# Fourier mixing and balanced experts: x in runs of four rows, table phases on GpSimd, the last fold and the weight turns in pieces, two more pauses, an earlier gather

## The chip, the cores and the metric

The kernel runs on one core of a Trainium2 chip. The metric is the time of one execution on the device in microseconds (us). The kernel before takes 534.44 us (median of three runs, 532.58 to 536.25). With one core there is no other core of the run to compare with, so a run counts as slow only where it is over 1.5% above the fastest of the same kernel in the same rounds; a single look (experiments 5, 6 and 10 to 12) has no known state. Ratios below are the mean time of one kernel's fast runs over that of the other's of the same rounds, so they are not quite the ratio of the medians that stand beside them.

The runs fell on several chips. On four occasions the kernel before took 534.4 to 535.6 us, on four others 585.9 to 591.9 us. In the traces that I compared PE is as busy on the second kind up to about 300 us and less busy after it: from 200 to 300 us it is busy for 97.17 us in experiment 1 on such a chip and 96.86 in the kernel before on one of the first kind, from 300 to 400 us 90.17 and 99.50, at a granted clock of 0.965 and 0.969 over the whole run. I call them quick and slow chips, use ratios within the same rounds alone, and read the first 172 us of profiles from either kind.

## The reference

```python
X = np.fft.fft(x, axis=1)            # x: (8, 2496, 256) float32
X = np.fft.fft(X, axis=2).real       # (19968 tokens, 256)
logits = X @ w_gate                  # 8 experts, each with room for 19968/8 tokens
# greedy: the largest logit first, one expert a token, no expert over its room
for idx in argsort(-logits.flatten()): ...
# per expert: out[mask] = relu(X[mask] @ w1[e]) @ w2[e]      (F = 1024)
```

## The kernel before

The transform is a product with cosine and sine tables. Rows s and S - s of x are added first (the fold), so that half a table is enough. The reversed rows come by indirect loads, which GpSimd issues. One pass of the loop below is a batch; the tables are built beside it, one of ten sets (cosine and sine) at a time. In the timelines below an engine takes its instructions in the order in which they stand in the program (DVE's eleven from 44.13 us on, in the prediction, do).

```python
def load_x(b):                               # three tiles of each kind
    ...                                      # forward rows, by SyncE, two rows (2 KiB) a piece
    for i in range(NK):                      # NK = 5 indirect loads a batch
        nc.gpsimd.indirect_dma_start(out=bv[0:n, i, :], in_=x_pairs, ...)

def phases(w, row, turns, period):           # angle r = k*row - period*round(k*turns)
    nc.vector.tensor_scalar(n1, in0=kgrid[:, 0:w], scalar1=turns, scalar2=MAGIC, ...)
    nc.vector.tensor_scalar(n1, in0=n1, scalar1=MAGIC, scalar2=-float(period), ...)
    nc.vector.scalar_tensor_tensor(r_t, in0=kgrid[:, 0:w], scalar=row, in1=n1, ...)

for b in range(B):                           # B = 8
    nc.vector.tensor_tensor(a_t[...], a_t[...], b_t[..., reversed], op=AL.add)   # the fold
    if b + 3 < B: load_x(b + 3)              # waits for the fold: same tile
    if b > 0: tab_waves()                    # ACT: Abs, Sin, cast to bf16 (hi) from r_t
    nc.scalar.copy(zb[:, :, 0:D:P], ...)
    nc.vector.tensor_tensor(zb[...], ...)    # the two additions into zball
    zts[b] = [turn_x(b, pv, 0), turn_x(b, pv, 1)]     # PE transposes, ACT copies them out
    if b > 0: gate_x(b - 1, ...)             # PE: gate matmuls of the batch before
    ...
    tab_low()                                # DVE: lo = tf - hi
    tab_phases()                             # the next set of phases
# then logits; choice of the experts beside the transforms; experts; out by indirect scatters
```

## Time and profile before

| stage of the profiled run before | us |
|---|---|
| start to start of last fold | 77.1 |
| last fold to first transform matmul | 23.4 |
| to first matmul of the experts | 71.5 |
| to the end of GpSimd's last scatter | 357.0 |
| to the end of the program | 5.2 |
| span | 534.3 |

### The profile page before, as it was taken

How to read it: one execution, taken by the hardware profiler on the slowest of the kernel's cores; microseconds unless marked ns; L12 is line 12 of the kernel's file. 1: busy time of each engine (PE TensorE's matmuls, PEld its weight loads, DVE VectorE, ACT ScalarE, POOL GpSimd, SP SyncE). 2: the span in 40 equal slices, each digit the busy share in tenths (PEclk: the TensorE clock that was granted, in tenths of full speed). 3: DMA queues.
4: the chain of work that ended last, by engine and by line, in shares of the span. 5: the costliest groups of instructions: out<-in, count | busy, mean ns of one | idle time of the engine just before them, and what ended most of it. 6: DMA issues, size and time to landing. Idle time of an engine off the chain costs nothing.

```text
span 534.3 us, 11232 instructions
## 1 busy us (share of the span) xinstructions
PE 471.8 (88%) x4039; PEld 357.7 (67%) x4039; DVE 372.7 (70%) x952; ACT 337.9 (63%) x762; POOL 313.9 (59%) x362
## 2 busy tenths in 40 slices
PE   0567659899789899999899999999999999999983
PEld 0544436776568566777667877777777777777753
DVE  7799994687978969889978757566654555555431
ACT  7879983156368778788767776556555555555531
POOL 7888815253122555555524336777677777777774
PEclk9968898999989999999989999999999999999988
DMA  8999929078578697523322323342222222222221
GB/s 259 317 281 319 310 89 159 2 240 291 140 217 261 161 225 163 137 95 103 99 76 100 99 88 102 113 130 85 82 83 78 79 87 84 79 69 78 77 77 53
DMA packets 35168, 74.62 MB, mean 140 GB/s; under 512 B 6115, under 2 KB 14349, under 8 KB 35104
## 3 DMA queue, kind: packets, MB, share of 16 engines
q0 software_dynamic: 23296, 42.10, 30.2%
q1 hardware_dynamic: 11808, 31.73, 17.7%
q8 instruction: 33, 0.54, 0.4%
q14 instruction: 31, 0.25, 0.2%
HBM read 51.26 MB, written 32.24 MB: 156 GB/s over the span
## 4 chain that ended last, share of the span: by engine, by line
PE 70%; DVE 13%; ACT 9%; issue 4%; DMA 3%; POOL 1%; POOLq 0%; DVEq 0%; ACTq 0%
PE hps L1234 24%; PE ops L1257 24%; PE sps L1098 5%; PE fftps L1038 5%; PE wps L1058 2%; PE tp L285 2%; ACT zt L287 2%; DMA xa<-in_x_dram 2%; PE yps L295 1%; ACT tf L254 1%; POOL out_dram L1261 1%; DVE xa L343 1%; PE inv_ps L766 1%; DVE stage L1022 1%; PE tp L1222 1%
## 5 line engine op out<-in xcount | busy, mean ns | idle before, releaser
L995 ACT ACTIVATE hb<-hps 128x384 bf16<-128x384 f32 (+1 forms) x326 | 146.2, 493 | 50.5 <-PE hps L1234 47.4
L1257 PE MATMUL ops<-w2t,hb 128*128 128x256 bf16 (+1 forms) x1344 | 175.3, 274 | 0.0
L1257 PEld LDWEIGHTS <-hb 128*128 128x128 bf16 (+1 forms) x1344 | 133.3, 100 | 32.6 <-issue 0.5
L1261 POOL DMA_INDIRECT out_dram<-zball,rid x85 | 89.3, 1051 | 82.7 <-ACT zball L995 63.8
L1234 PE MATMUL hps<-xs,zball 128*128 128x384 bf16 x640 | 127.3, 327 | 0.0
L1234 PEld LDWEIGHTS <-zball 128*128 128x128 bf16 x896 | 86.1, 98 | 43.4 <-issue 2.9
L999 DVE TENSOR_SCALAR hb<-hps 128x384 bf16<-128x384 f32 (+1 forms) x122 | 66.3, 549 | 47.2 <-PE hps L1234 39.2
L129 POOL DMA_INDIRECT xb<-in_x_dram,mir_i x40 | 54.3, 1357 | 11.9 <-issue 10.5
L995 ACT ACTIVATE zball<-ops 128x256 f32<-128x256 f32 (+1 forms) x79 | 30.4, 384 | 31.6 <-PE ops L1257 29.0
L1234 PE MATMUL hps<-xt,zball 128*128 128x384 bf16 (+1 forms) x256 | 48.4, 322 | 0.0
L285 PE MATMUL tp<-identf,xa 128*128 128x128 f32 x160 | 27.4, 336 | 20.1 <-issue 9.2
L285 PEld LDWEIGHTS tp<-identf,xa 128*128 128x128 f32 x160 | 23.6, 176 | 27.1 <-issue 10.2
L995 ACT ACTIVATE xs<-sps 128x384 bf16<-128x384 f32 x68 | 30.4, 493 | 16.0 <-PE sps L1098 15.7
L1026 POOL COPY stage<-stage 128x258 bf16<-128x258 bf16 x40 | 17.7, 447 | 36.3 <-DVE stage L1021 33.0
L1098 PE MATMUL sps<-pt,xl 128*128 128x192 bf16 x320 | 33.8, 246 | 0.7 <-DVE pt L1076 0.7
L1076 DVE TENSOR_SCALAR pt<-rampw,spot 128x193 bf16<-128x193 bf16 x160 | 32.5, 298 | 1.6 <-PE inv_ps L766 0.9
L1098 PEld LDWEIGHTS <-xl 128*128 128x128 bf16 x320 | 27.6, 98 | 3.5 <-issue 1.6
L1210 POOL DMA_INDIRECT xg<-t_dram,ids_l x24 | 23.1, 964 | 7.3 <-issue 7.3
L1261 POOL DMA_INDIRECT out_dram<-zball,rows_l x23 | 22.3, 969 | 7.3 <-issue 2.4
L1044 ACT COPY ev<-fftps 128x512 f32<-128x512 f32 x20 | 11.7, 584 | 22.9 <-PE fftps L1038 15.5
L1001 DVE COPY zball<-ops 128x256 f32<-128x256 f32 (+1 forms) x29 | 12.3, 424 | 19.4 <-PE ops L1257 19.4
L1024 ACT ACTIVATE stage<-stage 128x254 bf16<-128x254 bf16 x40 | 15.6, 414 | 13.3 <-DVE stage L1021 11.6
(356 smaller groups left out, 781.1 us busy)
## 6 DMA issues: line engine op xcount, KB each, us to landing
t_dram<-stage SPq DMA_DIRECT2D x20, 512.0 KB
xl<-t_dram SPq DMA_DIRECT2D x20, 512.0 KB
xa<-in_x_dram SPq DMA_DIRECT2D x8, 1024.0 KB
w1raw<-in_moe_w_dram POOLq DMA_DIRECT2D x8, 512.0 KB, 5.3
w2t<-in_moe_w_dram POOLq DMA_DIRECT2D x8, 512.0 KB, 6.3
xa<-in_x_dram SPq DMA_DIRECT2D x8, 224.0 KB
out_dram<-zball,rid POOLq DMA_INDIRECT x85, 2.5
xb<-in_x_dram,mir_i POOLq DMA_INDIRECT x40, 8.0
```

The lines of the kernel that those rows point to most:

```text
L129: nc.gpsimd.indirect_dma_start(out=bv[0:n, i, :], out_offset=None, in_=x_pairs, in_offset=bass.IndirectOffsetOnAxis(ap=mir_i[0:n, b * NK + ...
L285: nc.tensor.transpose(tp[:, blk, u, :], pv[:, 4 * c + u, blk * P:(blk + 1) * P], identf)
L995: nc.scalar.activation(dst, src, ACT.Relu if relu else ACT.Copy)
L999: nc.vector.tensor_scalar(dst, in0=src, scalar1=0.0, scalar2=None, op0=AL.max)
L1026: nc.gpsimd.tensor_copy(st[:, :, 1 + q, 0:P + 1], st[:, :, 3 * q, 0:P + 1])
L1038: nc.tensor.matmul(fps[:, :, d0:d1], lhsT=tab[:nv, i, ks], rhs=zball[:nv, b0:b0 + NB, 2 * i + r, d0:d1], start=(i == 0), stop=(i == NK - 1))
L1076: nc.vector.tensor_scalar(marks[n][:, f, 0:EW + 1], in0=rampw[:, 0:EW + 1], scalar1=spot[:, c:c + 1], scalar2=None, op0=AL.is_equal)
L1098: nc.tensor.matmul(sps[:, j2 * EW:(j2 + 1) * EW], lhsT=xl[:, 2 * g + cc, j2 * P:(j2 + 1) * P], rhs=pt[:, 2 * g + cc, 0:EW], start=(cc == 0 ...
L1210: nc.gpsimd.indirect_dma_start(out=xg[0:nr, q, :], out_offset=None, in_=t_dram, in_offset=bass.IndirectOffsetOnAxis(ap=d["ids"](q, nr), ax ...
L1234: nc.tensor.matmul(hps[:, 0:n], lhsT=w1t[d["e"]][:, j2, fc * P:(fc + 1) * P], rhs=d["x"](j2), start=(j2 == 0), stop=(j2 == 1))
L1257: nc.tensor.matmul(ops[0:nr, 0:D], lhsT=d["hid"][:, fc, b0:b0 + nr], rhs=w2t[d["e"]][:, fc, :], start=(fc == 0), stop=(fc == F // P - 1))
L1261: put = nc.gpsimd.indirect_dma_start(out=out, out_offset=bass.IndirectOffsetOnAxis(ap=d["rows"](b0 // P)[0:nr], axis=0), in_=ot[0:nr, :], ...
```

## The change

The intent is to unload the two fullest units of the first stage (DVE, and GpSimd with its loads), to take serial work from the last fold, and to remove single stops of PE later. The core of the diff:

```diff
+    x_quads = x.rearrange("b (s r) d -> (b s) (r d)", r=4)
-        for i in range(NK):
+        for i in range(3):                       # two of 128 runs of four rows, one of 112 pairs
...
-    def phases(w, row, turns, period):
+    def phases(w, row, turns, period, eng=nc.vector):
-        nc.vector.tensor_scalar(n1, ...)          # twice
+        eng.tensor_scalar(n1, ...)                # twice
+        if eng is nc.vector:
+            eng.scalar_tensor_tensor(r_t, ...)
+        else:
+            eng.tensor_scalar(r_t, in0=kgrid[:, 0:w], scalar1=row, scalar2=None, op0=AL.mult)
+            eng.tensor_tensor(r_t, r_t, n1, op=AL.add)
...
+                                         nc.vector if len(tabq) > 5 else nc.gpsimd)))   # last six sets
...
+        for g0, g1 in ((0, 4), (4, 8), (8, 2 * NK)) if b == B - 1 else ((0, 2 * NK),):   # last fold
...
+        if b == B - 1:
+            gate_x(b - 1, zts.pop(b - 1))         # ahead of the last transposes
...
-            if clock["n"] in (18, 22, 28, 34):
-                turn_w((18, 22, 28, 34).index(clock["n"]), "A")
+            if clock["n"] in TURNS:               # 16 places, one piece each
+                next(pieces)
...
+        yield SYNC                                # one more pause before count()
...
+        yield from settle(1)                      # and one in the first settling
...
-        while ... j >= min(max(placed[0] + 1 + m * (51 - placed[0]) // 15, ...), 38 + m):
+        while ... j >= min(max(placed[0] + 1 + m * (50 - placed[0]) // 15, ...), 37 + m):
```

More of the change, by code (lines that the diff above doesn't have):

```diff
@@ L104 @@
     ab = {}
-    mir_i = const.tile([P, B * NK], I32, name="mir_i")
-    nc.gpsimd.iota(mir_i.rearrange("p (b i) -> p b i", i=NK), pattern=[[S // 2, B], [-P, NK]],
-                   base=S // 2 - 2, channel_multiplier=-1)
+    mir_i = const.tile([P, B, 3], I32, name="mir_i")
+    nc.gpsimd.iota(mir_i[:, :, 0:2], pattern=[[S // 4, B], [-P, 2]], base=S // 4 - 2, channel_multiplier=-1)
+    nc.gpsimd.iota(mir_i[:, :, 2], pattern=[[S // 2, B]], base=S // 2 - 2 - 4 * P, channel_multiplier=-1)
     x_pairs = x.rearrange("b (s r) d -> (b s) (r d)", r=2)
+    x_quads = x.rearrange("b (s r) d -> (b s) (r d)", r=4)
+    m_int = const.tile([P, NK], I32, name="m_int")
     iota_p_i = const.tile([P, 1], I32, name="iota_p_i")
@@ L115 @@
     nc.gpsimd.iota(kgrid_i, pattern=[[1, KH]], base=0, channel_multiplier=0)
+    nc.gpsimd.iota(m_int[:, 0:4].rearrange("p (i h) -> p i h", h=2), pattern=[[2 * P, 2], [1, 2]], base=1,
+                   channel_multiplier=2)
+    nc.gpsimd.iota(m_int[:, 4:NK], pattern=[[0, 1]], base=4 * P + 1, channel_multiplier=1)
     def load_x(b):
         a_t = xap.tile([P, NK, 2, D], FT, tag="xa", bufs=3, name="xa")
-        b_t = xbp.tile([P, NK, 2, D], FT, tag="xb", bufs=3, name="xb")
-        av = a_t.rearrange("p i r d -> p i (r d)")
@@ L121, in load_x @@
-        bv = b_t.rearrange("p i r d -> p i (r d)")
-        nc.sync.dma_start(av[:, 0:NK - 1, :],
-                          x[b, 2:2 + 2 * P * (NK - 1), :].rearrange("(i p r) d -> p i (r d)", p=P, r=2))
-        m4 = 2 * (1 + P * (NK - 1))
-        nc.sync.dma_start(av[0:2 * HL, NK - 1, :], x[b, m4:m4 + 4 * HL, :].rearrange("(p r) d -> p (r d)", r=2))
-        nc.sync.dma_start(av[2 * HL:P, NK - 1, :], x[b, 0:32, :].rearrange("(p r) d -> p (r d)", r=2))
-        for i in range(NK):
-            n = P if i < NK - 1 else 2 * HL
-            nc.gpsimd.indirect_dma_start(
-                out=bv[0:n, i, :], out_offset=None, in_=x_pairs,
-                in_offset=bass.IndirectOffsetOnAxis(ap=mir_i[0:n, b * NK + i:b * NK + i + 1], axis=0),
-                element_offset=D)
@@ L133, in load_x @@
-        nc.sync.dma_start(bv[2 * HL + 1:P, NK - 1, :], x[b, 2:32, :].rearrange("(p r) d -> p (r d)", r=2))
-        nc.sync.dma_start(b_t[2 * HL:2 * HL + 1, NK - 1, 0, :], x[b, S - 1:S, :])
-        nc.sync.dma_start(b_t[2 * HL:2 * HL + 1, NK - 1, 1, :], x[b, 0:1, :])
+        b_t = xbp.tile([P, 2 * NK, D], FT, tag="xb", bufs=3, name="xb")
+        av = a_t.rearrange("p i r d -> p (i r d)")
+        bv = b_t.rearrange("p g d -> p (g d)")
+        nc.sync.dma_start(av[:, 0:8 * D].rearrange("p (i f) -> p i f", i=2),
+                          x[b, 2:2 + 8 * P, :].rearrange("(i p r) d -> p i (r d)", p=P, r=4))
@@ new lines, in load_x @@
+        m4 = 2 + 8 * P
+        nc.sync.dma_start(av[0:2 * HL, 8 * D:], x[b, m4:m4 + 4 * HL, :].rearrange("(p r) d -> p (r d)", r=2))
+        nc.sync.dma_start(av[2 * HL:P, 8 * D:], x[b, 0:32, :].rearrange("(p r) d -> p (r d)", r=2))
+        for i in range(3):
+            n = P if i < 2 else 2 * HL
+            nc.gpsimd.indirect_dma_start(
+                out=bv[0:n, (6 - 4 * i) * D:(10 - 4 * i) * D] if i < 2 else bv[0:n, 0:2 * D], out_offset=None,
+                in_=x_quads if i < 2 else x_pairs,
+                in_offset=bass.IndirectOffsetOnAxis(ap=mir_i[0:n, b, i:i + 1], axis=0),
+                element_offset=3 * D if i < 2 else D)
@@ L136, in load_x @@
+        nc.sync.dma_start(bv[2 * HL + 1:P, 0:2 * D], x[b, 2:32, :].rearrange("(p r) d -> p (r d)", r=2))
+        nc.sync.dma_start(b_t[2 * HL:2 * HL + 1, 0, :], x[b, S - 1:S, :])
+        nc.sync.dma_start(b_t[2 * HL:2 * HL + 1, 1, :], x[b, 0:1, :])
         ab[b] = (a_t, b_t)
@@ L147 @@
     m_cols = const.tile([P, NK], FT, name="m_cols")
-    nc.vector.tensor_scalar(m_cols, in0=kgrid[:, 0:NK], scalar1=float(P), scalar2=iota_p, op0=AL.mult, op1=AL.add)
-    nc.vector.tensor_scalar(m_cols, in0=m_cols, scalar1=1.0, scalar2=None, op0=AL.add)
+    nc.vector.tensor_copy(m_cols, m_int)
     below = const.tile([P, 1], FT, name="below")
@@ L187, in masks @@
         nc.vector.tensor_scalar(skip, in0=skip, scalar1=1.0, scalar2=None, op0=AL.add)
-    def phases(w, row, turns, period):
+    def phases(w, row, turns, period, eng=nc.vector):
         n1 = early.tile([P, KH], FT, tag="n1", bufs=2, name="n1")[:, :w]
-        nc.vector.tensor_scalar(n1, in0=kgrid[:, 0:w], scalar1=turns, scalar2=MAGIC, op0=AL.mult, op1=AL.add)
-        nc.vector.tensor_scalar(n1, in0=n1, scalar1=MAGIC, scalar2=-float(period), op0=AL.subtract, op1=AL.mult)
+        eng.tensor_scalar(n1, in0=kgrid[:, 0:w], scalar1=turns, scalar2=MAGIC, op0=AL.mult, op1=AL.add)
+        eng.tensor_scalar(n1, in0=n1, scalar1=MAGIC, scalar2=-float(period), op0=AL.subtract, op1=AL.mult)
         r_t = early.tile([P, KH], FT, tag="rt", bufs=2, name="rt")[:, :w]
-        nc.vector.scalar_tensor_tensor(r_t, in0=kgrid[:, 0:w], scalar=row, in1=n1, op0=AL.mult, op1=AL.add)
+        if eng is nc.vector:
+            eng.scalar_tensor_tensor(r_t, in0=kgrid[:, 0:w], scalar=row, in1=n1, op0=AL.mult, op1=AL.add)
+        else:
+            eng.tensor_scalar(r_t, in0=kgrid[:, 0:w], scalar1=row, scalar2=None, op0=AL.mult)
+            eng.tensor_tensor(r_t, r_t, n1, op=AL.add)
         return r_t
@@ L242, in tab_phases @@
             i, r = tabq.pop(0)
-            open_p.append((i, r, phases(KH, rows_t[:, r, i:i + 1], turns_t[:, r, i:i + 1], S // 2 * (1 + r))))
+            open_p.append((i, r, phases(KH, rows_t[:, r, i:i + 1], turns_t[:, r, i:i + 1], S // 2 * (1 + r),
+                                         nc.vector if len(tabq) > 5 else nc.gpsimd)))
     def tab_waves():
@@ L291, in gate_x @@
         yps = psl.tile([P, 4, P], FT, tag="y", bufs=2, name="yps")
-        for blk in range(2):
-            for c, zt in enumerate(zts):
+        for c, zt in enumerate(zts):
+            for blk in range(2):
                 nn = 4 if c < 2 else 2
@@ L342 @@
         a_t, b_t = ab.pop(b)
-        nc.vector.tensor_tensor(a_t[:, :, :, 1:D], a_t[:, :, :, 1:D], b_t[:, :, ::-1, D - 1:0:-1], op=AL.add)
-        nc.vector.tensor_tensor(a_t[:, :, :, 0], a_t[:, :, :, 0], b_t[:, :, ::-1, 0], op=AL.add)
+        av = a_t.rearrange("p i r d -> p (i r) d")
+        for g0, g1 in ((0, 4), (4, 8), (8, 2 * NK)) if b == B - 1 else ((0, 2 * NK),):
+            bv = b_t[:, 9 - g0:(9 - g1 if g1 < 2 * NK else None):-1, :]
+            nc.vector.tensor_tensor(av[:, g0:g1, 1:D], av[:, g0:g1, 1:D], bv[:, :, D - 1:0:-1], op=AL.add)
+            nc.vector.tensor_tensor(av[:, g0:g1, 0], av[:, g0:g1, 0], bv[:, :, 0], op=AL.add)
         if b + 3 < B:
@@ L362 @@
         nc.vector.tensor_tensor(zb[:, :, P + 1:D], pv[:, :, 1:P], pv[:, :, D - 1:P:-1], op=AL.subtract)
+        if b == B - 1:
+            gate_x(b - 1, zts.pop(b - 1))
         zts[b] = [turn_x(b, pv, 0), turn_x(b, pv, 1)]
-        if b > 0:
+        if 0 < b < B - 1:
             gate_x(b - 1, zts.pop(b - 1))
@@ L661, in search, with settle @@
             found["low"], found["wid"] = low2, wid2
-    def settle():
+    def settle(more=0):
         low, wid, lo0, ltf = found["low"], found["wid"], found["lo0"], found["ltf"]
@@ L687, in settle @@
         yield 1.6
-        yield SYNC
+        for _ in range(1 + more):
+            yield SYNC
         bps = misc()
@@ L902, in choose_rest @@
         yield SYNC
+        yield SYNC
         count()
@@ L924, in settle_rest @@
     def settle_rest():
-        yield from settle()
+        yield from settle(1)
         for _ in range(NROUND - 1):
@@ L1052, in turn_w, with turn_pieces @@
     def turn_w(e, eng=None):
+        for _ in turn_pieces(e, eng):
+            pass
+    def turn_pieces(e, eng=None):
         for j in range(2):
@@ L1060, in turn_w @@
                 take(w1t[e][:, j, fs], wps, eng=eng)
-        if e + 2 < E:
-            load_w1(e + 2)
+                if j == 1 and fh == 1 and e + 2 < E:
+                    load_w1(e + 2)
+                yield
     flat = [zball[:, b].rearrange("p i d -> p (i d)") for b in range(B)]
@@ L1134, in sort_rows_sum @@
         busy["D"] += 0.4
+    TURNS = (*range(15, 23), *range(26, 30), *range(33, 37))
+    pieces = (None for e in range(4) for _ in turn_pieces(e, "A"))
     units = (cost for n in range(4 * NT) for cost in transform(n))
@@ L1144, in unit @@
             clock["n"] += 1
-            if clock["n"] in (18, 22, 28, 34):
-                turn_w((18, 22, 28, 34).index(clock["n"]), "A")
-                clock["PE"] += 2.0
+            if clock["n"] in TURNS:
+                next(pieces)
+                clock["PE"] += 0.45
         return cost is not None
@@ L1323, in feed @@
             settled(j)
-        while m < len(late) and placed and j >= min(max(placed[0] + 1 + m * (51 - placed[0]) // 15, 0 if m < 8 else 32), 38 + m):
+        while m < len(late) and placed and j >= min(max(placed[0] + 1 + m * (50 - placed[0]) // 15, 0 if m < 8 else 32), 37 + m):
             gather(late[m])
```

## The prediction

> **What bounds the kernel now.** I first read the busy tenths, which split the 534.3 us into stages. From 0 to about 90 us x is loaded, folded and turned, and the cosine tables are built. From 90 to 100 us come the logits, from 100 to 172 us the transforms beside the first choice, from 172 us to the end the experts. In the last stage PE is at 9 in nearly every slice.
>
> ```profile
> PE   0567659899789899999899999999999999999983
> DVE  7799994687978969889978757566654555555431
> POOL 7888815253122555555524336777677777777774
> DMA  8999929078578697523322323342222222222221
> ```
>
> Before 75 us the third to sixth digit of DVE and of DMA are all 9, so PE's share says nothing there. I opened the timeline of DVE for one batch of that stage.
>
> ```profile
> 44.13 2.81 DVE L343 TENSOR_TENSOR xa<-xa,xb 128x2550 f32<-128x2550 f32 x1
> 46.86 0.17 DVE L344 TENSOR_TENSOR xa<-xa,xb 128x10 f32<-128x10 f32 x1
> 46.95 0.32 DVE L309 TENSOR_TENSOR yhl<-ytp,yhl 128x160 bf16<-128x160 f32 x1
> 47.18 1.47 DVE L361 TENSOR_TENSOR zball<-xa 128x1270 bf16<-128x1270 f32 x1
> 48.57 1.47 DVE L362 TENSOR_TENSOR zball<-xa 128x1270 bf16<-128x1270 f32 x1
> 49.96 0.48 DVE L271 TENSOR_TENSOR lo_cE<-tf,hi_cE 128x313 bf16<-128x313 f32 x1
> 50.36 0.48 DVE L271 TENSOR_TENSOR lo_sE<-tf,hi_sE 128x313 bf16<-128x313 f32 x1
> 50.75 0.37 DVE L191 TENSOR_SCALAR n<-kgrid,turns_t 128x313 f32<-128x313 f32 x1
> 51.16 0.34 DVE L192 TENSOR_SCALAR n<-n 128x313 f32<-128x313 f32 x1
> 51.54 0.55 DVE L194 SCALAR_TENSOR_TENSOR rt<-kgrid,rows_t,n 128x313 f32<-128x313 f32 x1
> 52.04 2.81 DVE L343 TENSOR_TENSOR xa<-xa,xb 128x2550 f32<-128x2550 f32 x1
> ```
>
> From one fold to the next is 52.04 - 44.13 = 7.91 us without a hole, so DVE sets the pace; the last three rows, the table phases, take 52.04 - 50.75 = 1.29 us of it. DMA is nearly as full (share 1.02 from 10 to 68 us, 310 GB/s), and GpSimd is 8.5 us of 10 busy issuing five indirect loads a batch. The folds start at 16.26, 28.14, 35.87, 44.13, 52.04, 59.96, 68.83 and 77.09 us; the logits start at 90.41, 13.3 us after the last fold, a stretch with nothing to overlap.
>
> The view of waits gives PE's stops later on; the timeline of GpSimd gives the end.
>
> ```profile
> 148.33 0.59 PE L1058 MATMUL wps<-w1raw,mt_b 128*128 128x512 bf16 x2 [2.11 <-ACT zball L995]
> PE misc L601 <- DVE dd L594: 2.7, 1, 2.7
> PE misc L690 <- DVE trun L686: 2.1, 1, 2.1
> PE tp L1222 <- DMA xs<-t_dram,ids_l: 2.3, 2, 1.4
> 524.31 0.97 POOL L1261 DMA_INDIRECT out_dram<-zball,rows_l  x1 [0.55 <-DVE zball L1001]
> 525.58 0.97 POOL L1261 DMA_INDIRECT out_dram<-zball,rows_l  x1 [0.30 <-issue]
> 526.85 0.97 POOL L1261 DMA_INDIRECT out_dram<-zball,rows_l  x1 [0.30 <-issue]
> ```
>
> The first four are single stops of a PE that otherwise never waits after 150 us: evictions of a burst of weight turns, the count of the last choice, the first settling, the last gather. The last three show GpSimd issuing one scatter each 1.27 us; going back through its timeline there is no larger hole from 387 to 524 us. So the end is bound by GpSimd's issue, with PE only just as late.
>
> [...]
>
> ```profile
> 36.24 3.27 POOL L129 DMA_INDIRECT xb<-in_x_dram,mir_i  x1 [0.30 <-issue]
> ```
>
> This load, normally 0.95 us, lies under the fold of 35.87 to 38.68 us and ends 0.83 us after it. In the other direction no reading GpSimd operation stands in front of a fold here; the nearest thing is one phase instruction on DVE at 23.24 us that took 0.86 us in place of 0.38 beside a row of GpSimd memsets. [...] The trace has one-input copies: 258 elements in 0.41 us and 1024 in 1.04, so 0.82 ns an element and 0.20 us fixed[...]; a two-input one is not there. [...] Here the 2 KiB loads run at 310 GB/s with the engines full; the stage stores, 4 KiB a row, make a 126 us window of 419 GB/s. [...] Here the 16 transposes take 1.94 us at full clock and 2.92 after the idle time before the last batch.
>
> **The change part by part.**
>
> (1) Runs of four rows. The x loads, 20.4 MB, go from 2 KiB to 4 KiB pieces; indirect loads fall from 40 to 24. At an estimated 365 GB/s (the 3.6 KB hardware packets between 105 and 130 us took 63% of 16 engines for 25 us over 1584 packets, 159 ns each) loading needs 56 us in place of 66. GpSimd saves 2 x 1.3 = 2.6 us a batch. Neither is the pace of a batch, since DVE already is, so by itself I give this part 0 to 1 us; it buys slack.
>
> (2) Phases on GpSimd. The order of the built program shows six of ten phase sets moving off DVE. The first falls where DVE waits for ACT anyway (1.75 us before its fold of 28.14), so five count: 5 x 1.29 = 6.5 us less DVE work. But each becomes four GpSimd instructions: three of 0.20 + 313 x 0.82 ns = 0.46 us[...]. Nearly all of DVE's batch is two-input work from SBUF. If the lock holds both ways, each wedges between two DVE instructions[...]. If it does not, the pace falls to ACT's, about 7.0 us a batch (26.9 us busy in 30 us, 8.9 of each 10, times 7.91), and this saves 5 x 0.9 = 4.5 us and something of the batch pair with 8.87 us. I take two thirds for the lock: 2/3 x 0 + 1/3 x 5 = about 1.5 us saved, for (1) and (2) together.
>
> (3) Last fold in three pieces and the gate of batch 6 moved ahead of it. Now: transposes at 80.09, both gates after them, logits at 90.41. Then: the gate matmuls of batch 6 (1.9 to 2.6 us) run at 77.9 under the fold, whose first piece is done 1.2 us after 77.09; transposes from about 79.9 to 83, copies by ACT (1.0, 1.0, 0.6) to about 84.4, the last gate to 85, its copies, transposes and the low part 2.2 us more: logits near 87.2. Gain 3.2 us, all on the path.
>
> (4) Weight turns in single pieces: same 32 matmuls, but no burst of four overruns the three PSUM buffers. Goes: 2.11 and 0.46 us of waits, and about 1.6 us of slowed matmuls after the long one (148.8 to 152.7 took 3.9 us for work that takes 2.2). The chain of the choice now has 21 transform units beside it in place of 24, so its own waits of 1.29, 0.99 and 0.53 us may grow by a few tenths. Gain 3 us.
>
> (5) Two more pauses. Each puts one more pacing step, about 1.85 us of matmuls (six of hps and eight of ops), ahead of the stop. 2.1 and 2.7 become about 0.2 and 0.5. In the built program the index is finished at the same tile (20) in both. Gain 4 us.
>
> (6) Gathers. Run through the new formula, only the sixteenth moves, one tile earlier, ahead of three scatters (3.8 us), more than the 2.3 us PE waits for it. But GpSimd issues the same number of instructions back to back; only its 0.55 us hole goes. Gain 0.6 us.
>
> Sum: 1.5 + 3.2 + 3 + 4 + 0.6 = 12.3 us; with half a microsecond for the shorter head, 534.4 - 12.9 = 521.5 us.
>
> **The rivals.** A: the lock makes the first stage slower. DVE's folds stand back to back, so any blocking costs at once: a batch of 8.4 to 9.0 us, five times 0.5 to 1.1 more, the last fold at 80 to 82 us; total near 527 to 530. For it: the stretched load above. Against it: 40 reading indirect loads did not stretch one fold (2.807 to 2.817 us). B: the first stage is really held by DMA and the five indirect loads, and DVE only follows. For it: the fold at 68.83 came as x landed (the chain names a DMA of 8.47 us there). Then (1) and (2) bring 7 to 9 us, total near 514. Against it: no hole of DVE in the batches before. C: the pauses and pieces only move the waits: DVE, 9.4 of 10 busy from 170 to 190 us, is as late at the next stop. Then (4) and (5) bring 3 in place of 7 us, total near 526.
>
> **Range and chances.** The certain parts, (3) and about half of (4) to (6), give 7 us; A against B spreads the head by -3 to +7, C by 4. I take 513 to 529 us. The 2% line is 523.7, 2.2 us above my number with a spread of about 6 to either side: faster 0.62, within 2% 0.37, slower 0.01.
>
> **What would show it.** Right: logits near 87 us or earlier; no wait of PE for an eviction of wps; waits at the two counts under 1 us; no wait for the last gather, GpSimd still back to back at the end. (2) is judged by the time between folds 2 to 6 (7.9 now; over 8.2 is rival A, under 7.2 is B) and by whether folds or zball additions last longer than 2.81 and 1.47 us. Wrong would be a new hole of PE over 3 us after 100 us, or indexes late at tile 20.

The forecast: 1.5 + 3.2 + 3 + 4 + 0.6 = 12.3 us, and with the half a microsecond for the head 521.5 us in all. Of the 1.5 us for parts (1) and (2), the 0 in "2/3 x 0" stands as the author's estimate, as do the two thirds and rival A's sizes; the 5 us beside it come from the traces. What it calls the lock is, as far as this case shows it, the hold of the load at 36.24 us: 3.27 us in place of 0.95 under a fold.

## More of the kernel before

The prediction shows the main lines. One more is needed: the windows view of 44 to 60 us. Its columns are the stretch, its length, busy time with number of instructions of PE, PE's weight loads, DVE, ACT and GpSimd (POOL), then PE's granted clock, the share of the DMA engines and GB/s.

```profile
44.00:60.00 16.00, 12.12 (x76) 7.99 (x76) 15.86 (x22) 15.77 (x35) 13.56 (x9) 0.89 1.03 307
```

DVE, ACT and the DMA engines are all full at once, and GpSimd has 2.4 us of 16 left.

## The result

The changed kernel is slower: 553.86 us (median of four, 553.45 to 554.21) against 535.30 us for the kernel before in the same rounds, ratio 1.0355 with a 95% interval of 1.0313 to 1.0397. Both profiles fell on quick chips, the granted clock of PE is 0.969 before and 0.962 after, and so they can be laid side by side:

| stage | before | after | difference |
|---|---|---|---|
| start to start of last fold | 77.09 | 92.25 | +15.2 |
| last fold to first transform matmul | 23.45 | 21.82 | -1.6 |
| to first matmul of the experts | 71.54 | 69.98 | -1.6 |
| to the end of GpSimd's last scatter | 356.98 | 354.37 | -2.6 |
| to the end of the program | 5.24 | 13.03 | +7.8 |
| span | 534.3 | 551.5 | +17.2 |

Two rows make the loss, and the prediction's sum had neither: the first stage, of which rival A had 3 to 5 us, and the close of the program after the last scatter. These are the busy tenths of the page of after (40 slices of 13.8 us, each digit tenths of the slice):

```profile
PE   0575667779699999999999999999999999999950
DVE  8695568488887998779888766556555555555520
POOL 7569892453232284536453436777777777777770
DMA  8996650909658799523222223332222222222120
```

In the slices of 41 to 83 us (the fourth to sixth digit) DVE has fallen to 5, 5, 6 and DMA to 6, 6, 5, where DVE stood at 9 in all three before, and DMA at 9, 9, 2 (the prediction misread that last digit as a 9); GpSimd (POOL) has risen to 9, 8, 9. The last slice is empty on all engines: that is the close. The window of 44 to 60 us says the same, PE's clock included (0.63):

```profile
44.00:60.00 16.00, 8.45 (x37) 5.51 (x38) 9.55 (x10) 11.42 (x25) 14.28 (x11) 0.63 0.64 209
```

The timeline of DVE for one batch after (start, duration, engine, line, operation, tiles, and in brackets the idle time before it with what ended it):

```profile
46.27 2.81 DVE L356 TENSOR_TENSOR xa<-xa,xb 128x2550 f32<-128x2550 f32 x1
...
50.47 0.32 DVE L319 TENSOR_TENSOR yhl<-ytp,yhl 128x160 bf16<-128x160 f32 x1 [1.30 <-ACT yhl L318]
50.72 1.47 DVE L374 TENSOR_TENSOR zball<-xa 128x1270 bf16<-128x1270 f32 x1
52.10 1.47 DVE L375 TENSOR_TENSOR zball<-xa 128x1270 bf16<-128x1270 f32 x1
56.98 0.49 DVE L281 TENSOR_TENSOR lo_cE<-tf,hi_cE 128x313 bf16<-128x313 f32 x1 [3.40 <-ACT hi_cE L268]
...
58.24 2.82 DVE L356 TENSOR_TENSOR xa<-xa,xb 128x2550 f32<-128x2550 f32 x1
```

From fold to fold it is 58.24 - 46.27 = 11.97 us, not 7.91, and no DVE instruction is longer than before. DVE waits: 3.40 us for a cast by ACT. ACT in turn sat idle for 4.07 us until GpSimd's last phase instruction. The timeline of GpSimd in the same batch:

```profile
46.18 1.00 POOL L134 DMA_INDIRECT xb<-in_x_dram,mir_i  x1 [0.30 <-issue]
47.23 2.27 POOL L196 TENSOR_SCALAR n<-kgrid,turns_t 128x313 f32<-128x313 f32 x1
49.59 1.31 POOL L197 TENSOR_SCALAR n<-n 128x313 f32<-128x313 f32 x1
50.98 3.46 POOL L202 TENSOR_SCALAR rt<-kgrid,rows_t 128x313 f32<-128x313 f32 x1
54.53 0.85 POOL L203 TENSOR_TENSOR rt<-rt,n 128x313 f32<-128x313 f32 x1
55.52 1.04 POOL L134 DMA_INDIRECT xb<-in_x_dram,mir_i  x1
```

GpSimd has no hole. The set lasts from 47.23 to 55.38, 8.15 us; the one at 23.63 us, beside an idle DVE, took 0.53 + 1.32 + 1.08 + 0.84 = 3.8 us. L196 ends at 49.50, 0.42 us after the fold, and L202 at 54.44, 0.87 us after the second zball addition: it wasn't let in between the two additions. Then come the three loads of the next batch (55.52 to 59.15, 3.6 us), and the next set begins under the next fold. So 8.15 + 3.6 us and the short gaps make up the 12 us.

Not every instruction of a set is held through both additions. In the traces of the changed kernel, of its repeat and of experiments 2, 3, 5 and 6, the first and the third instruction of a set, which read a factor from a tile, started under the first addition 17 times in all, and each time they ended after the second. The second and the fourth did so 6 times and were let in each time; the second addition then took 1.71 to 2.13 us in place of 1.47.

The close shows in no view, because a drain isn't counted as work. These are the trace's own records of GpSimd at the end, start and duration:

```
before   529.06  end of the last scatter       after   538.42  end of the last scatter
         531.12  0.60  counter update                  539.63  2.30  counter update
         531.74  1.71  DRAIN                           541.96  8.65  DRAIN
         534.30  end of the span                       551.45  end of the span
```

From the waits after, of PE (total, times, longest): the eviction wait on wps and the 2.7 us wait at a count are gone, the settling (2.1 before) waits 0.8, and the wait for the last gather is gone too. But the chain of the choice waits more:

```profile
PE lev_ps L855 <- DVE stage L1039: 3.1, 1, 3.1
PE fftps L1055 <- DVE stage L1039: 2.9, 3, 1.5
...
PE misc L706 <- DVE trun L701: 0.8, 1, 0.8
```

### The profile page after: what moved, and what is told of

Same layout as the page of the kernel before. It is cut to its first block, busy times and chain, and to the rows that moved or that the text cites. A ratio compares the mean times of both kernels' runs of the same rounds, so it can differ in the third digit from the quotient of the medians.

```text
span 551.5 us, 11226 instructions
## 1 busy us (share of the span) xinstructions
PE 472.4 (86%) x4039; PEld 360.2 (65%) x4039; DVE 368.1 (67%) x937; ACT 337.5 (61%) x762; POOL 328.5 (60%) x373
## 4 chain that ended last, share of the span: by engine, by line
PE 62%; DVE 16%; DMA 7%; POOL 6%; issue 3%; ACT 3%; SPq 0%; POOLq 0%; DVEq 0%; ACTq 0%
PE hps L1258 23%; PE ops L1281 22%; PE fftps L1055 5%; DMA xa<-in_x_dram 5%; PE sps L1120 4%; PE wps L1079 2%; DVE pt L1098 2%; POOL xb L134 2%; DMA xb<-in_x_dram 2%; DVE xa L356 2%; POOL rt L203 1%; POOL rt L202 1%; PE tp L1246 1%; PE inv_ps L782 1%; POOL n L197 1%
## 5 line engine op out<-in xcount | busy, mean ns | idle before, releaser
L1285 POOL DMA_INDIRECT out_dram<-zball,rid x85 | 91.1, 1071 | 79.7 <-ACT zball L1012 57.9
L295 PE MATMUL tp<-identf,xa 128*128 128x128 f32 x160 | 32.3, 377 | 27.2 <-ACT zt L297 16.5
L295 PEld LDWEIGHTS tp<-identf,xa 128*128 128x128 f32 x160 | 27.5, 198 | 34.6 <-ACT zt L297 22.1
L134 POOL DMA_INDIRECT xb<-in_x_dram,mir_i x24 | 28.2, 1176 | 14.3 <-DVE xa L357 8.2
L1120 PEld LDWEIGHTS <-xl 128*128 128x128 bf16 x320 | 27.7, 98 | 3.5 <-issue 1.0
L1061 ACT COPY ev<-fftps 128x512 f32<-128x512 f32 x20 | 11.7, 583 | 21.9 <-PE fftps L1055 12.4
L1285 POOL DMA_INDIRECT out_dram<-wa,rid x20 | 19.8, 988 | 6.1 <-issue 3.4
```

Source lines behind the costliest of these rows:

```text
L134: nc.gpsimd.indirect_dma_start(out=bv[0:n, (6 - 4 * i) * D:(10 - 4 * i) * D] if i < 2 else bv[0:n, 0:2 * D], out_offset=None, in_=x_quads ...
L295: nc.tensor.transpose(tp[:, blk, u, :], pv[:, 4 * c + u, blk * P:(blk + 1) * P], identf)
L1120: nc.tensor.matmul(sps[:, j2 * EW:(j2 + 1) * EW], lhsT=xl[:, 2 * g + cc, j2 * P:(j2 + 1) * P], rhs=pt[:, 2 * g + cc, 0:EW], start=(cc == 0 ...
L1285: put = nc.gpsimd.indirect_dma_start(out=out, out_offset=bass.IndirectOffsetOnAxis(ap=d["rows"](b0 // P)[0:nr], axis=0), in_=ot[0:nr, :], ...
```

## The experiments

My theory after the result: GpSimd's queue has become the bound of the first stage, because its phase instructions are held while DVE runs instructions with two inputs from SBUF (L196 took 2.27 us in place of 0.53, L202 3.46 in place of 1.08), and ACT waits behind them (4.07 us). The rivals: the four-row loads land late; DVE itself is slowed; the wait is one of latency alone and GpSimd has time enough.

### 1. All phases back on DVE

```diff
-                                         nc.vector if len(tabq) > 5 else nc.gpsimd)))
+                                         nc.vector)))
```

> The changed kernel with all ten sets of table phases back on DVE; everything else of the change stays. Theory (GpSimd's queue is the new bound of the first stage: three loads at 1.3 us and a set of phases of 8.2 us, held under DVE's two-input instructions, make the 12 us from fold to fold): the folds come 7.8 to 8.1 us apart again, the last one at 76 to 78 us in place of 92.3, and the time falls by about 15 us, to 537 to 541 us. Rival 1 (the four-row loads land later and hold the folds): folds stay 10 us apart or more, total over 545 us. In either case what is left over 524 us is not the phases but a part of the change after the logits.

Measured on a slow chip: 585.46 us against 585.92, ratio 1.0025 (0.9946 to 1.0104), where the changed kernel has 1.0355. The folds are 7.9 us apart again, the last one starts at 76.97 us, and the logits at 87.24:

```profile
43.11 2.81 DVE L356 TENSOR_TENSOR xa<-xa,xb 128x2550 f32<-128x2550 f32 x1
...
50.98 2.81 DVE L356 TENSOR_TENSOR xa<-xa,xb 128x2550 f32<-128x2550 f32 x1
```

92.25 - 76.97 = 15.3 us come from the phases, and the four-row loads are cleared as their cause. The close is still long: drain 8.65 us.

### 2. Only the phases on GpSimd

The kernel before with the diff's lines on `phases` and nothing else.

> The kernel before with nothing but the last six sets of phases on GpSimd; loads stay in two-row pieces, five a batch. Theory (GpSimd's queue full): 5 x 1.3 + 8.2 = 14.7 us from fold to fold where all five loads and a set fall into a batch, last fold near 100 us, total 553 to 562 us. Rival 1 (four-row loads are what delays): folds stay near 8 us apart, total within 3 us of before. Rival 2 (DVE itself slowed[...]): folds and zball additions take longer than 2.81 and 1.47 us, and DVE has no holes; 8.5 to 9 us a batch, total 537 to 541.

Measured: 615.69 us against 585.92 (no ratio, since two of its four runs count as slow). Folds 13.8 to 14.4 us apart from the third to the seventh, the last one at 108.06 us, fold duration unchanged at 2.82. With five loads in the queue in place of three it is worse, as the theory has it; 14.7 us a batch and a last fold near 100 us were expected. The close is short here: drain 1.71 us.

### 3. The phase instructions a second time, for nobody

```diff
+            if len(tabq) <= 5:
+                idle_set(i, r)      # the same four GpSimd instructions, into a part of zball not yet in use
```

> All phases on DVE, and in the places where the change puts its GpSimd sets the same four GpSimd instructions once more, whose results nobody reads. It separates GpSimd's queue from ACT's wait for the phases. Theory (queue full): the spare sets are held as before (8 us a set), the loads behind them go out late, and the folds are 11 to 12.5 us apart, total within 5 us of the changed kernel (549 to 556). Rival 3 (the trouble is only that ACT, in order, waits for the phases, while GpSimd has time enough): with nobody waiting the folds come 8 us apart, total as in the run with the phases on DVE. Either way x is still loaded three batches ahead, so some lateness of loads can be absorbed: 8 to 9 us a batch would mean the wait of ACT is the larger half.

Measured: the last fold at 81.92 us, 5 us later than in experiment 1; folds 8.3 to 10.1 us apart from the third on. The time, 597.32 us (1.0199, 1.0112 to 1.0287), is inflated by my edit: the additions of the last batch had to wait 2.71 us for my spare set, which used their place. So I read this run up to the last fold only. With nobody waiting for their results, the sets cost 5 us here, a third of the 15.3. That the rest is ACT's wait for the results is not shown by it: GpSimd fell behind in this run, with spare sets that start at 36.01, 50.77, 66.12 and 77.44 us, 11.3 to 15.4 us apart, and loads that are issued three batches ahead can hide such a lag in a stage of eight batches. Experiment 5 tests it. The run also shows the hold in the other direction:

```profile
43.53 1.02 DVE L196 TENSOR_SCALAR n<-kgrid,turns_t 128x313 f32<-128x313 f32 x1
...
58.37 2.13 DVE L385 TENSOR_TENSOR zball<-xa 128x1270 bf16<-128x1270 f32 x1
```

The first is 0.38 us elsewhere, the second 1.47: in both places a GpSimd instruction was under way first (from 43.52 and 57.45 us), and DVE waited. This is the prediction's rival A at its true size, 8.3 and 8.8 us in the two batches without other waits. In the changed kernel, where DVE waits for ACT (3.40 us in the batch shown), the two additions of one batch (1.70 and 1.71 us in place of 1.47) and one short piece of a fold (0.81 in place of 0.17) lasted longer.

### 4. Twelve memsets in place of the spare set

> As the run before this one, but the spare instructions on GpSimd are twelve memsets of 128x313, estimated 0.3 us each from 0.28 us for 128x160, together about 3.7 us, which is what a set of phases takes unheld (0.53+1.28+1.08+0.84); a memset reads no SBUF. Theory (GpSimd instructions that read SBUF are held while DVE runs a two-input instruction): the memsets last the same under a fold as beside it, a batch of GpSimd is 3.9 + 3.7 = 7.6 us, folds 7.9 to 8.3 us apart, total within 3 us of the run with the phases on DVE. If memsets are held too, they last up to 3.4 us under folds and this run is as slow as the spare reading one. If plain occupation of GpSimd mattered, held or not, this run too would be slow.

Measured: 584.45 us (0.9986, 0.9885 to 1.0086), folds 7.9 us apart for the most part, the last one at 77.15. The memsets' durations, minimum, median and maximum in ns over 72:

```profile
L211 POOL MEMSET zball<- x72: 361/362/562, 23.5 to 77.4; 128x313 f32 x72
```

Twelve memsets, which occupy GpSimd for 4.87 and 5.00 us in the two batches from 35.32 and 46.74 us and read no SBUF, cost nothing that shows (the last fold at 77.15 us, 76.97 in experiment 1) and aren't held (0.562 us at most). Of the two kinds of instruction tried, the hold is seen on the phases, which read SBUF, and not on these.

### 5. One batch ahead

```diff
             tab_phases()
+            tab_phases()            # at the end of batch 0: every later GpSimd set a batch earlier
```

> The changed kernel with GpSimd's sets of phases issued one batch earlier (one more set at the end of batch 0, so that every later one has a whole batch more before ACT needs it). The spare reading run cost 5 us at the last fold with nobody waiting for the results, the changed kernel 15.3 us; the other 10 are ACT's wait. Theory A (GpSimd has too little time: three loads at 1.3 us and a held set of about 8 us are 12 us a batch, so being a batch ahead helps once only): the first two folds after batch 2 come 8 to 9.5 us apart, the later ones 11 to 12 again, last fold at 84 to 88 us. Theory B (a wait of latency alone, fold to phases to ACT to fold): with a batch of room the folds come 8.3 to 9.5 us apart as in the spare reading run, last fold at 80 to 82.5 us.

On a quick chip: 551.49 us against 534.80. The folds after 27.93 come 7.1 and 7.3 us apart, then 11.4 to 13.2, the last one at 90.15 (84 to 88 was expected). Theory A it is: the lead was eaten in two batches, after which GpSimd, with no hole over 0.42 us from 27.7 to 83.7 us, set the pace again. A fold was held here, too, 3.36 us in place of 2.81, while a GpSimd instruction recorded from 42.48 to 43.02 us ran at its unheld 0.54:

```profile
42.33 3.36 DVE L356 TENSOR_TENSOR xa<-xa,xb 128x2550 f32<-128x2550 f32 x1
```

### 6. Every other set on GpSimd

```diff
-                                         nc.vector if len(tabq) > 5 else nc.gpsimd)))
+                                         nc.gpsimd if len(tabq) in (4, 2, 0) else nc.vector)))
```

> The changed kernel with only every other set on GpSimd (three in place of six: 6th, 8th and 10th), the others on DVE. GpSimd then has two batches for two times three loads and one set, 7.8 + 8 = 16 us, about the 15.8 us that DVE needs for two. Theory A (GpSimd's time is what runs short): folds 7.9 to 8.8 us apart, last fold at 77 to 80 us, near the 76.97 us of the run with all phases on DVE. Theory B (each set on GpSimd costs its latency in its own batch): the three batches concerned still take 11 to 12 us, last fold at 85 to 89 us.

547.69 us against 534.80, the last fold at 85.63 us. That is theory B's range, and I had expected A's. GpSimd has holes here, and still DVE waits for what comes through it:

```profile
51.51 0.95 POOL L134 DMA_INDIRECT xb<-in_x_dram,mir_i  x1 [3.50 <-DVE xa L357]
...
45.85 0.49 DVE L281 TENSOR_TENSOR lo_cO<-tf,hi_cO 128x313 bf16<-128x313 f32 x1 [5.44 <-ACT hi_cO L268]
```

The first two batches with a GpSimd set take 14.4 and 12.9 us, the one between them 6.8. So both are true: with six sets GpSimd is full, and with three it isn't, but a set queued behind loads that wait for the fold, and then held by the fold and the additions, comes too late for its own batch. To move fewer sets isn't the cure.

### 7. Only the four-row loads

The changed kernel with everything else undone.

> Of the whole change only the x loads in runs of four rows (24 indirect loads in place of 40); all else as before. In the profiles so far the last act of the program, GpSimd's closing drain, took 1.71 us in the kernel before and in the one with only the phases on GpSimd, but 8.65 us in the changed kernel and in all made from it, and the counter instruction ahead of it 0.60 and 2.30 us: from the last scatter to the end 5.2 and 6.9 us against 13.1 to 14.0. Theory: the four-row loads, which change the number and size of GpSimd's transfers, cause that; then this kernel ends 13 to 14 us after its last scatter, the folds stay 7.9 us apart, the last one at 76.5 to 77.5 us, and the total is 6 to 8.5 us above before. Rival: the closing stretch depends on something else of the change (pieces of the weight turns, program length); then it is 5 to 7 us here and the total within 1 us of before.

Measured on a slow chip: 587.62 us, ratio 1.0006 (0.9918 to 1.0093); the expected total isn't confirmed, within an interval of 0.9% to either side. The profile is clear: the last fold at 76.23 us, 0.9 us earlier than before; x comes at 325 GB/s between 10 and 58 us, against 311; and the close takes 13.9 us with a drain of 8.65.

### 8. Everything but the four-row loads and the GpSimd phases

> The mirror of the last run: the changed kernel without the four-row loads and without phases on GpSimd, so last fold in pieces, gate moved, weight turns in pieces, two pauses, gather formula. Theory: closing drain 1.71 us and 5 to 7 us from the last scatter to the end; logits at about 87.2 us as in the run with the phases on DVE; no wait for evictions of weight turns and under 1 us at the two counts; total 6 to 9 us below before, which would make it the best so far. Rival: if the drain comes from these parts it lasts 8.65 us here and the total is within 2 us of before.

Measured on a slow chip: 584.82 us, ratio 0.9982 (0.9891 to 1.0074), no gain that the interval shows. Close 5.8 us, drain 1.71. Together with 7 this settles that the four-row loads lengthen the close.

### 9. The same number of GpSimd transfers

Experiment 1 with two one-row loads of each batch issued by GpSimd in place of SyncE.

> The changed kernel with the phases on DVE and, in each batch, the two one-row loads issued by GpSimd in place of SyncE: GpSimd's number of transfers is then again that of the kernel before (24 + 16 loads), its bytes hardly change. If the closing drain depends on the number of GpSimd's transfers, it is 1.71 us again and the total 6 to 9 us below the run with the phases on DVE, measured against before. If it depends on the rows or bytes that they moved, it stays 8.65 us or takes a third value. GpSimd's batch is 3 x 1.3 + 2 x about 1.0 = 5.9 us, so the folds should stay 7.9 us apart.

Measured: 590.34 us, ratio 1.0077 (0.9987 to 1.0166). A third value: drain 9.47, counter 2.50 us. The number of transfers alone, 272 as before, isn't what counts.

### 10. The same 16 small transfers on top of two-row loads

> The kernel with two-row loads and all the later parts of the change (it closed with counter 0.59 and drain 1.71 us), with the two one-row loads of each batch issued by GpSimd: 16 more small GpSimd transfers. With four-row loads the same 16 made counter and drain 0.2 and 0.82 us longer. If the drain follows how far GpSimd's transfers have filled some fixed store since it last wrapped, it is 0.79 and 2.5 us here, the same steps. If it depends on whether four-row pieces occur at all, it stays 0.59 and 1.71 us.

On a quick chip: 536.06 us against 534.80; counter 0.60, drain 1.71, unchanged. The step of 0.82 us didn't repeat, so the rule as I had put it is wrong in this place. The last fold starts at 81.45 us here, 4.4 us later than before; why wasn't looked into.

### 11. Two padding gathers a batch

```diff
+        for i in range(2):
+            nc.gpsimd.indirect_dma_start(out=spare[:, b, i, :], in_=x_quads, ...)   # 128 rows of 32 bytes, never read
```

> The changed kernel with the phases on DVE (closing counter 2.30, drain 8.65 us) and two more GpSimd gathers a batch, 128 rows of 32 bytes each, into a spare tile that nobody reads: 16 more transfers, 40 gathers in all as in the kernel before, and as many rows as the four-row loads saved. If the drain follows the fill of a store that wraps, and a row counts once whatever its length, counter and drain are back at 0.59 and 1.71 us. If they only grow with the number of rows moved, they are longer than 2.5 and 9.5 us. If four-row pieces by themselves make them long, they stay about 2.3 and 8.65 us. The head may lose a few us to the extra gathers (5 x 1.3 = 6.5 us of GpSimd a batch, as before); only the close is read here.

On a quick chip: 529.87 us against 534.80. Counter 0.59, drain 1.71 us, the folds 7.9 us apart as without padding. More transfers made the close 8.6 us shorter: it isn't the four-row pieces as such.

### 12. One padding gather a batch

> As the run with two more gathers a batch (closing drain 1.71 us), but with one more gather a batch only: 8 in all. If the drain follows the fill of a store that wraps, then from the two changes seen [...] drain 10.3 to 10.7, counter 2.7 to 2.8 us, longer than without any padding, although twice the padding made it short. If it were a plain matter of the number of transfers (short at 256 + 16 or more), it would lie between 8.65 and 1.71 us.

Drain 0.89, counter 0.40 us, where I had expected over 10. My rule for the size is wrong; the count of entries that it used is shown by no run. On a slow chip: 589.64 us against 591.88, 0.4% less.

### 13. Only pieces and pauses, twice

> The kernel before with only the weight turns in pieces and the two more pauses. The prediction gave them 3 + 4 = 7 us. Its rival C (waits only move) gave 3. Theory from the two traces: the transforms gain about 1.7 us (71.6 to 69.95 us from first transform to first expert matmul) and the experts 2.7 us up to GpSimd's last scatter, because from about 390 us GpSimd issues back to back and what PE gains after that does not count: total 3.5 to 5 us below before, closing drain 1.71 us, PE's waits of 2.1, 2.7 and 2.1 us gone or under 1 us.

> The kernel before with only the weight turns in pieces and the two more pauses, repeated. If the end is bound by GpSimd's issue from about 390 us on and only what is gained ahead of that counts: 3.5 to 5 us below before, ratio 0.990 to 0.994. If the prediction's sizes hold: 7 us, ratio 0.987. If the waits only moved (rival C): 3 us or less, ratio 0.994 or more.

The first fell on a slow chip, 583.43 us, ratio 0.9932 (0.9845 to 1.0020). The repeat on a quick chip: 534.11 us against 535.63, ratio 0.9974 (0.9935 to 1.0014), so 1.4 us less, with some 2 us to either side. That is rival C's range, and it leaves out the 7 us of the prediction; the first interval, wider, does not leave them out. The waits of PE in the repeat:

```profile
PE lev_ps L840 <- DVE stage L1024: 3.1, 1, 3.1
...
PE tp L1231 <- DMA xs<-t_dram,ids_l: 2.3, 2, 1.3
```

### 14. Repeats, timed

> The changed kernel itself once more, for the same rounds as the two below: ratio to before 1.033 to 1.038, drain 8.65 us, last fold at 91.5 to 93 us.

Ratio 1.0338 (1.0284 to 1.0392) on a slow chip, with the last fold at 92.78 us and a drain of 8.65. The loss is the same on both kinds of chip.

> The changed kernel with the phases on DVE and two padding gathers a batch, timed: 529.9 us in one look against 534.8 of before. Expected from its profile: ratio 0.988 to 0.993, so 4 to 6 us below before, drain 1.71 us, logits at 87.2 us.

590.67 us, ratio 0.9977 (0.9916 to 1.0037). On this slow chip the gain of experiment 11 didn't show.

> The changed kernel without four-row loads and without phases on GpSimd, on a chip where the end is bound by GpSimd. From the parts: logits 2.5 to 3 us earlier than before, about 1.7 us less in the transforms, about 2.7 us less from the first expert matmul to GpSimd's last scatter, perhaps 1.9 us more from logits to transforms (seen in all runs but that of before), drain 1.71 us: total 5 to 7 us below before, ratio 0.987 to 0.991, level with the padded four-row version.

594.05 us, ratio 1.0034 (0.9978 to 1.0090): no gain on a slow chip.

> The changed kernel with the phases on DVE and one padding gather a batch, timed. On a chip where before takes about 535 us: drain 0.89 us and a close of about 5 us; logits at 86.5 to 87.5 us (3 to 3.5 us earlier than before), 2 to 3.5 us gained after them: total 4 to 6.5 us below before, ratio 0.988 to 0.993. On a chip of 586 us or more, where PE sets the end: ratio 0.993 to 1.000.

579.14 us against 586.95 on a slow chip, ratio 0.9861 (0.9830 to 0.9891). This version, the one of experiment 12, with four-row loads, all phases on DVE, all later parts and one padding gather a batch, is the only one that beats both kernels by more than the noise, though not by 2%. It was timed on one chip, and the single look of experiment 12, on another slow chip, was only 0.4% below before.

What the slow chips do, in the window of 400 to 500 us, first for the changed kernel on a quick chip, then for experiment 1 on a slow one:

```profile
400.00:500.00 100.00, 100.00 (x818) 77.02 (x817) 53.07 (x106) 54.36 (x112) 76.22 (x79) 1.00 0.24 81
```

```profile
400.00:500.00 100.00, 81.55 (x627) 59.71 (x626) 38.04 (x78) 38.74 (x86) 64.01 (x66) 0.98 0.20 68
```

PE is busy for 81.55 us of 100 with the clock still at 0.98. Its holes have no releaser that the profile knows. The cause wasn't looked for.

## Why the prediction was wrong

The prediction said 521.5 us, 513 to 529; it was 553.86. By its own steps:

**(2), phases on GpSimd, is the step that failed.** It had it that each set "wedges between two DVE instructions", at a cost to DVE that was an estimate, and so set 0 us with two thirds and 5 us saved with one third. The runs show a loss of 15.3 us (experiment 1). Three things were missing. First, DVE mostly wins: it is GpSimd that is held, and a set takes 8.15 us in place of 3.8. Second, GpSimd's own budget wasn't worked out: the prediction freed 2 x 1.3 us of GpSimd and called it slack, then gave it a set of phases without adding up. Three loads and a held set are 12 us. Third, the result goes on to ACT, then to DVE ahead of the next fold, so the delay is on the path; experiment 6 shows this even where GpSimd has holes. The unheld set was mis-sized as well: it takes 3.8 us, since the first scaling takes 0.53 us, the second 1.32 and the third 1.08, not 0.46 each, and the addition 0.84. Rival A named the lock and saw only its smaller side (8.3 to 8.8 us a batch, experiment 3). None of the rivals reached 12.

**(1), four-row loads**: 0 to 1 us was right for the first stage (0.9 us, experiment 7), but the estimate of 365 GB/s wasn't reached, 325. (The "126 us window of 419 GB/s" beside it stands in no view: 419 is the rate of single slices of 0.6 us between 105 and 130 us, a stretch whose mean is 239. And at the end of the sum, 12.3 and half a microsecond are 12.8, not 12.9.) What the prediction didn't see at all is the close: 7.8 us longer. Experiments 7, 8 and 11 show that the set of GpSimd's transfers decides it. By what rule stays open. The drains seen are 0.89, 1.71, 8.65 and 9.47 us; with 272 transfers it was 1.71 in two forms of the program and 9.47 in a third, and eight added gathers shortened it where a store that fills steadily should have lengthened it. Nor does the number of packets on GpSimd's queue decide it: with 23296 of them the drain was 1.71 us (before) and 0.89 (experiment 12), with 23552 it was 1.71 (experiment 11) and 9.47 (experiment 9). My guess of a store that wraps early would fit experiments 11 and 12, not experiment 10, and isn't shown.

**(3), last fold in pieces**: 3.2 us predicted, and the logits at 87.24 us in experiment 1 where 87.2 was predicted look like a hit. They are one only in part. From the last fold to the logits the profile of before shows 13.32 us, but 11.7 in four other runs with an unbroken last fold (experiments 2, 7 and both of 13), against 9.8 to 10.3 in most runs with pieces. The 1.6 us between 13.32 and 11.7 are PE's granted clock: before had 0.5 from 80.9 to 84.3 us, and its 16 transposes took 2.92 us and the next 12 gate matmuls 2.56, where the four others, at full clock there, have 1.94 and 1.91. And the 10.1 us from logits to transforms in that one profile are 11.5 to 12.1 in the others: all 19 other traces have a hole of PE of 1.2 to 1.7 us within the logits, ahead of lps_cO, for which the profile knows no releaser, and that of before has none. From last fold to first transform, where the two happen to cancel, it is 23.3 to 23.5 us unbroken, 21.5 to 22.2 in most runs with pieces and 22.9 to 23.3 in four of them (experiments 4, 9, 10 and the repeat of 11). So the gain is mostly 1.1 to 2.0 us: the mechanism right, the size read from a single profile that happened to be at half clock there. The four runs that gain less are at half clock in the same stretch: their moved gate falls into a stretch of 3.4 us with a granted clock of 0.5, which begins at 77.6, 77.7, 81.8 and 77.9 us, and takes 3.4 to 3.6 us in place of 1.9.

**(4), weight turns in pieces**: 3 us predicted, about 0 found. From first transform to first expert matmul the runs with turns in bursts take 69.9 us (experiments 2 and 7), the ones of experiment 13 take 70.0; the 71.5 of the profile before is again its own. The 1.6 us of slowed matmuls, which the prediction put down to the long wait, ran at a granted clock of 0.5 from 149.1 to 152.6 us; experiments 2 and 7 have the same wait of 2.1 us, at full clock and without the slowed matmuls. The wait of 2.1 us for an eviction went, and that of lev_ps rose from 1.3 to 3.1, of fftps on stage from 2.1 to 2.9. The prediction expected "a few tenths" there. Rival C was right.

**(5) and (6), pauses and gather**: 4 and 0.6 us predicted. The waits at the count and the settling did go (2.7 to nothing, 2.1 to 0.8), and new ones of 1.0 us and less came up. From first expert matmul to the last scatter it is 354.3 to 354.8 us in six quick runs with the pauses, against 357.0 in the one quick profile without them: 2.2 to 2.7 us. The prediction itself had said that GpSimd issues back to back from 387 us on and that the end is bound by it. PE's gain after that point can't count; PE ended 2.9 us ahead of GpSimd before and 7.0 us ahead after. For the gather, 0.5 us at most is left (354.8 without it, 354.3 to 354.7 with it).

Of the tests that the prediction named, "over 8.2 is rival A" fired, for another reason than rival A; fold and addition durations stayed at 2.81 and 1.47 with one batch at 1.71, which spoke against rival A and rightly so; and a new PE hole of over 3 us after 100 us was there (3.1).

## What to carry to other kernels

Before work goes to another engine, add up that engine's batch with what it already issues, and follow its result to whoever waits for it: an engine that looks 85% busy with loads that it merely issues is no place for a link of the main chain. On GpSimd count an SBUF-reading instruction beside folds and additions like these at the time for which DVE held it and its own length, not at its own alone: 3.46 us here for one of 1.08. Look at the close of the program in the trace's records when GpSimd's transfers change: here it cost 7.8 us, where all the later parts gained 5.8 in the same two profiles. And don't take a gain's size from one profile: two of the predicted sizes held 1.6 us each that were PE's half clock in that one execution.
